# Fifteen early score operands in the weight slots, and layer 2's preparation in its written order

## Chip, core and metric

The kernel runs on one core of a Trainium2 chip. The metric is the device time of one execution in microseconds (us); a matrix engine (TensorE, PE in the rows), a vector engine (VectorE, DVE), a scalar engine (ScalarE, ACT) and the DMA queue of SyncE (SP) do the work.

## What is computed

Windowed attention with 32 global tokens, then two feed-forward layers on the 2304 resulting tokens of width 512:

```
s_l  = scale * q_l @ k_l.T masked to |i - j| <= 32, and scale * q_l @ k_g.T beside it
a_l  = softmax(s_l);  out_l = a_l @ [v_g, v_l];  out_g the same over all keys
x    = [out_g, out_l], heads side by side                        # 2304 x 512
h    = x @ w_in                                                  # 512 x 2048
g    = h where h >= 1, 0 where h <= -1, (h + 1)^2 / 4 between
x1   = g @ w_out                                                 # 2048 x 512
out  = ((x1 @ w_a) * (x1 @ w_b)) @ w_out2                        # 512 x 1536, 1536 x 512
```

The weights arrive as 64-bit numbers. Every factor of the two layers is split into a high and a low part, so that each product takes three matmuls (high by high, low by high, high by low).

## The kernel before

**Attention.** The tokens are cut into 18 blocks of 128, and the work on them into items (one block, one pair of heads); three items make a group (`Local`). For an item a transfer brings `qk` (176 KB; L176) and one brings `v` (256 KB; L183). A group goes through scores on TensorE (`s_pe`, L203), minimum on VectorE (L218), exponential on ScalarE (L223), sum and reciprocal (`recip`, L230, L231), scaling (`scale`: one half on ScalarE, L239, one on VectorE, L240), transposition (`t_pe`, L246, copied at L248) and the product with `v` (`v_pe`, L257).

**Layer 1.** Three blocks make a tile, so there are six. A unit (t, f) of tile t and one of 16 strips of the hidden width has an `h_unit` (matmuls `hp`, L587 to L589; ScalarE L915; VectorE L916, L917; the split of the gate at L920, L921) and an `x_unit` (matmuls into four `acc` banks on the same lines). A raw weight strip (`wraw`, 512 KB, loaded at L101) is turned into fp32 at L109 (ScalarE), L110 and L111 (VectorE), and split at L118 (high part, ScalarE) and L119 (low part, VectorE; L117 to L119 are the general `split`). Strips are named i0, i1, ... for `w_in` and o0, o1, ... for `w_out`, used in the order i0, i1, o0, i2, o1, ...

**The start.** `begin` asks for the first transfers in the order of a string, `EARLY`: k is the next item's `qk`, v its `v`, w the next raw weight strip. All of them go to SP's queue, but for two `qk`. The pool of 32 slots called "w" holds split weights; at the start they are empty, and raw weights as well as the first twelve `qk` and `v` live in them (`EARLY_ITEMS`). Later items use pools of their own, so that item 12's `qk` and those behind it need a buffer of `qk`, and item 17's needs one that group 4's scores give back. Then `begin` runs groups 0 to 3 (tile 0), and the scores of group 4. The first six units of layer 1 on tile 0 (`FA`) run while tile 1's groups, 4 and on, go through attention between them.

**Layer 2.** Three stages s of 12 units; unit u = 12 s + f. Units 0 to 23 are `ab_unit`s: seven products k = 0 to 6 of three-matmul sums each (`prod`, L777 to L780), of which 0, 2, 4 and 5 go into bank `pb` and 1, 3 and 6 into bank `px`. VectorE and ScalarE take them out: L806 reads product 1, L816 and L817 products 4 and 3, L821 the last of `pb`, L825 product 6, L826 ends the second half. Product 0 of the next unit can't begin before L821 is done, product 3 not before L806, product 6 not before L817. Between products come fills: matmuls of the output layer for the unit before (`y_block`, bank `py`).

`side(u)` is called behind each product and prepares what comes: the loads `x1_load` for the next stage (at f = 1), `x_pre` (L646, L647; at f = 10, k = 6), `x_op` with its splits (at f = 11, one per k, L658 and L661 within), the sums of weights `ab_sum` (L686 to L689) and their splits `ab_split` for the next unit, the load `ab_load` for the one after, `y_prep` (a conversion and a split, in stage 0), and in stage 1 `yw_load`, `yw_sum` (L758 to L761, tile `yq`) and `yw_split` (tile `yo`). A scheduler places the instructions on each engine; it takes what it thinks ready first, and may so lift a step ahead of work that was written before it. `tc.issue_after(i)` keeps everything inside it behind instruction i.

Of the kernel before, what the change touches and what calls it, by code (L numbers as in the profile page):

```python
# [46 lines left out]

WARM = 6
START_GROUPS = 4
EARLY_ITEMS = 12  # L50
EARLY = "kkkkkkkkkvvvkkkwvvvwvvvwkkkvvvwkkvvvwwvvww"
FA = 6
LEAD1 = 2

# [8 lines left out]
QKBUFS = 5  # L63
# [5 lines left out]
def body(tc, qk, vw, kg, vg, vt, w1i, w1o, w2a, w2b, w2o, mask, eye, out):  # L69
    nc = tc.nc  # L70
# [24 lines left out]
    def w_load(key, src):  # L95
        if len(wraws) < EARLY.count("w"):
            raw = wp.tile([P, 512, 2], I32, name="wraw0", tag="w", bufs=32)
        else:
            raw = sp["p"].tile([P, 512, 2], I32, name="wraw", bufs=sp["raw"])
        wraws.append(key)  # L100
        nc.sync.dma_start(raw, src.bitcast(I32).rearrange("p (f two) -> p f two", two=2))  # L101
        wq.append((key, raw))
# [60 lines left out]
    class Item:  # L163
# [4 lines left out]
        def load(self):  # L168
            n = nat["n"]
            nat["n"] += 1  # L170
            if n < EARLY_ITEMS:
                self.qk = wp.tile([P, QK], F32, name="qk0", tag="w", bufs=32)
            else:
                self.qk = gp["k"].tile([P, QK], F32, name="qk", tag="qk", bufs=QKBUFS)
            queue = nc.scalar if n in (1, 3) else nc.sync
            queue.dma_start(self.qk, qk[self.blk, self.p])  # L176

        def load_v(self):
            if ld["v"] < EARLY_ITEMS:
                self.v = wp.tile([P, NQ, P], F32, name="v0", tag="w", bufs=32)  # L180
            else:
                self.v = ap.tile([P, NQ, P], F32, name="v", tag="v", bufs=VBUFS)
            nc.sync.dma_start(self.v, vw[self.blk, self.p])  # L183
# [187 lines left out]
    for t, blks in enumerate(TILES):  # L371
        loc = [(j, blk) for j, blk in enumerate(blks) if blk != GLOB]
        its = [Item(j, blk, p) for p in range(NPAIR) for j, blk in loc]
        n = len(loc) if len(loc) > 1 else 2
# [4 lines left out]
    ld = {"k": 0, "v": 0, "s_done": 0, "v_done": 0, "vb": 0, "g": 0}  # L379
    flat_items = [(g, it) for g in groups for it in g.items]  # L380
    first_glob = next(n for n, (g, it) in enumerate(flat_items) if isinstance(g, Glob))
# [12 lines left out]
    def load_v():  # L394
        g, it = flat_items[ld["v"]]
        it.load_v()
        ld["v"] += 1
        ld["vb"] += (ld["v"] > EARLY_ITEMS) + isinstance(g, Glob)

    def may_k():  # L400
        n = ld["k"]
        if n >= len(flat_items):
            return False
        if n >= first_glob:
            return "p" in gp and ld["s_done"] >= n
        return n < max(EARLY_ITEMS, ld["s_done"]) + QKBUFS

    def may_v():
        n = ld["v"]
        if n >= len(flat_items):  # L410
            return False
        need = (n >= EARLY_ITEMS) + (n >= first_glob)
        return (n < first_glob or "p" in gp) and ld["vb"] + need <= VBUFS

    def loads():
# [77 lines left out]
    def begin():  # L493
        for kind in EARLY:
            {"k": load_k, "v": load_v, "w": lambda: W1.load_to(W1.li + 1)}[kind]()
        n = START_GROUPS
        g = groups
        s_part(g[0])
        g[0].s_post()
        s_part(g[1])  # L500
        fill(WARM)
        low = []
        for k in range(n + 1):
            if k:
                for i in range(3):
                    g[k - 1].t_pe(i)
            if k + 1 < n:
                g[k + 1].s_post()
            if k + 2 < n:
                s_part(g[k + 2])  # L510
            if pend:
                low.pop()()
                w_end()
            if k < n:
                g[k].recip()
                g[k].scale()
            if k:
                v_part(g[k - 1])
                if k < n:
                    fill(WARM)  # L520
                else:
                    s_part(g[n])
                g[k - 1].v_post()
            if low:
                low.pop()()
            if k:
                low.append(x_chunk(0, k - 1, widths(0)))
            if k == n - 1:
                w_begin()
        low.pop()()  # L530
        w_begin()
        g[n].s_post()
        w_end()
# [4 lines left out]
    for g, grp in enumerate(groups):  # L538
        if g < START_GROUPS:
            continue  # L540
        n = grp.nt if isinstance(grp, Local) else 1
# [80 lines left out]
    def x1_load(s):  # L622
        n = half_cols(s)
        t0, t1 = PAIRS[s]
        w0 = widths(t0)
        for h in range(2):
            for c in range(NC):
                r = mp.tile([P, 384], F32, name=f"x1r{h}{c}", tag=f"xh{c}" if h else f"xraw{c}", bufs=1)
                lo, hi = h * n, (h + 1) * n
                if lo < w0:  # L630
                    e = min(hi, w0)
                    nc.sync.dma_start(r[:, :e - lo], x1d[t0][c, :, lo:e])
                if hi > w0:
                    b0 = max(lo, w0)
                    nc.sync.dma_start(r[:, b0 - lo:n], x1d[t1][c, :, b0 - w0:hi - w0])
                if s == 0 and h == 0:
                    q = t_tile("part", c % 2, c // 2)
                    nc.sync.dma_start(q, part[c])
                    nc.vector.tensor_tensor(r, r, q, ALU.add)
                xr[(h, c)] = r  # L640

    def x_pre(s):
        n = half_cols(s)
        for c in range(2):
            t1, t2 = t_tile("t1", c, 0), t_tile("t2", c, 1)
            nc.vector.tensor_tensor(t1[:, :n], xr[(1, c)][:, :n], xr[(0, c)][:, :n], ALU.subtract)  # L646
            nc.vector.tensor_tensor(t2[:, :n], xr[(1, 2 + c)][:, :n], t1[:, :n], ALU.subtract)  # L647
            tt[(1, c)], tt[(2, c)] = t1, t2

    def x_op(s, k):  # L650
        n = half_cols(s)
        if len(xo) <= k:
            xo.append((slot(), slot()))
        hi, lo = xo[k]
        for c in range(2):
            if k == 4:
                t3 = t_tile("t3", c, 0)
                nc.vector.tensor_tensor(t3[:, :n], xr[(1, 2 + c)][:, :n], xr[(1, c)][:, :n], ALU.subtract)  # L658
                tt[(3, c)] = t3
            if k == 5:  # L660
                nc.vector.tensor_tensor(tt[(2, c)][:, :n], xr[(0, 2 + c)][:, :n], tt[(2, c)][:, :n], ALU.subtract)  # L661
            src = [xr.get((0, c)), xr.get((0, 2 + c)), tt.get((2, c)), tt.get((1, c)), tt.get((3, c)),
                   tt.get((2, c)), xr.get((1, 2 + c))][k]
            split(hi[:, c, :n], lo[:, c, :n], src[:, :n])
# [15 lines left out]
    def ab_sum(u):  # L680
        if (u, 2) in wt:
            return
        a, b = wt[(u, 0)], wt[(u, 1)]
        q = sp["p"].tile([P, 4, 256], F32, name="wsum", bufs=1)
        h0, h1 = slice(0, 256), slice(256, 512)
        nc.vector.tensor_tensor(q[:, 1], b[:, h0], b[:, h1], ALU.add)  # L686
        nc.vector.tensor_tensor(q[:, 0], q[:, 1], a[:, h0], ALU.subtract)
        nc.vector.tensor_tensor(q[:, 2], a[:, h0], b[:, h0], ALU.subtract)
        nc.vector.tensor_tensor(q[:, 3], a[:, h1], q[:, 0], ALU.subtract)  # L689
        wt[(u, 2)] = q  # L690
        if u < U1:
            nc.sync.dma_start(wqd[u], q.rearrange("p a b -> p (a b)"))
# [43 lines left out]
    def y_prep(f):  # L736
        key, t = w2_conv()
        assert key == ("y", f)
        nc.sync.dma_start(yd[f // 2][:, f % 2], t)
        w = slot()  # L740
        split(w[:, 0], w[:, 1], t)
        wslots[key] = w
# [220 lines left out]
    for u in range(len(units)):  # L963
        for kind in (0, 1):
            if kind == 0:
# [17 lines left out]
                if u in conv_at:  # L983
                    i = conv_at.index(u)
# [58 lines left out]
    def side(u):  # L1043
        s, f = divmod(u, NF2)

        def run(k):
            if f == 1 and k == 0:
                x1_load(s + 1)
            if f == NF2 - 2 and k == 6:
                x_pre(s + 1)  # L1050
            if f == NF2 - 1:
                x_op(s + 1, k)
            if u > 0:
                if k == 1:
                    ab_sum(u + 1)
                elif 2 <= k < 6:
                    ab_split(u + 1, k - 2)
            if k == 6 and u + 2 not in (U1 + 1, U2 + 1):
                ab_load(u + 2)
            if k == 4 and s == 0:  # L1060
                y_prep(f)
            if s == 1:
                c = f // 2
                if f % 2 == 0:
                    if k == 0 and f == 0:
                        yw_load(0)
                    elif k == 6:
                        yw_sum(c)
                        if c < 5:
                            yw_load(c + 1)  # L1070
                elif k in (2, 5):
                    yw_split(c, k // 3)
        return run
# [19 lines left out]
    n = half_cols(2)  # L1093
# [235 lines left out]
```

## Time and profile before

| | us |
|---|---|
| three runs | 895.35, 899.59, 900.65 (median 899.59) |
| the profiled run | 902.1 |
| its span, first to last instruction | 900.3 |
| TensorE busy | 879.7 (98%) |
| VectorE busy | 633.8 (70%) |
| ScalarE busy | 488.9 (54%) |

The mean granted clock of TensorE is 0.991 of full speed. Busy times are of the profiled run; they overlap between engines, so the time is read from the engine that is waited for, and from what it waits for.

### The profile page before, as it was taken

How to read it: one execution, taken by the hardware profiler on the slowest of the kernel's cores; microseconds unless marked ns; L12 is line 12 of the kernel's file. 1: busy time of each engine (PE TensorE's matmuls, PEld its weight loads, DVE VectorE, ACT ScalarE, POOL GpSimd, SP SyncE). 2: the span in 40 equal slices, each digit the busy share in tenths (PEclk: the TensorE clock that was granted, in tenths of full speed). 3: DMA queues.
4: the chain of work that ended last, by engine and by line, in shares of the span. 5: the costliest groups of instructions: out<-in, count | busy, mean ns of one | idle time of the engine just before them, and what ended most of it. 6: DMA issues, size and time to landing. Idle time of an engine off the chain costs nothing.

```text
span 900.3 us, 19284 instructions
## 1 busy us (share of the span) xinstructions
PE 879.7 (98%) x7322; PEld 831.9 (92%) x7322; DVE 633.8 (70%) x1590; ACT 488.9 (54%) x1195; POOL 0.3 (0%) x5
## 2 busy tenths in 40 slices
PE   8699999999999999999999999999999999999998
PEld 6589999999999999988999999999989899999998
DVE  6599897666556655555488687776978668676683
ACT  6588676545445444443455555555745446555442
POOL 0000000000000000000000000000000000000000
PEclk9789999999999999999999999999999999999999
DMA  9948667855444532344282564533598521644531
GB/s 316 362 139 269 185 212 243 263 179 188 159 141 129 177 111 88 121 137 146 88 282 80 161 190 155 163 118 110 171 325 273 197 82 36 205 137 130 182 120 54
DMA packets 77612, 153.59 MB, mean 171 GB/s; under 512 B 9296, under 2 KB 35792, under 8 KB 77520
## 3 DMA queue, kind: packets, MB, share of 16 engines
q1 hardware_dynamic: 76944, 151.85, 51.8%
q8 instruction: 57, 0.93, 0.4%
q10 hardware_dynamic: 576, 0.52, 0.2%
q14 instruction: 35, 0.29, 0.1%
HBM read 119.05 MB, written 33.29 MB: 169 GB/s over the span
## 4 chain that ended last, share of the span: by engine, by line
PE 83%; DMA 8%; ACT 4%; DVE 3%; issue 1%; SPq 1%; ACTq 0%; DVEq 0%
PE hp L587 6%; PE acc L587 6%; PE acc L588 6%; PE acc L589 6%; PE hp L588 6%; PE hp L589 6%; PE pb L777 4%; PE pb L779 4%; PE pb L780 4%; PE py L844 3%; PE py L845 3%; PE px L777 3%; PE py L843 3%; PE px L779 3%; PE px L780 3%; DMA wraw<-in_w1i_dram 3%
## 5 line engine op out<-in xcount | busy, mean ns | idle before, releaser
L587 PE MATMUL hp<-xh,w 128*128 128x384 f32 (+1 forms) x384 | 131.9, 344 | 0.5 <-DVE m L916 0.4
L587 PE MATMUL acc<-g,w 128*128 128x384 f32 (+1 forms) x384 | 127.4, 335 | 1.7 <-ACT g L920 1.1
L588 PE MATMUL hp<-xh,w 128*128 128x384 f32 (+1 forms) x384 | 126.8, 330 | 1.0 <-DVE w L119 1.0
L589 PE MATMUL hp<-xl,w 128*128 128x384 f32 (+1 forms) x384 | 126.6, 330 | 0.0
L588 PE MATMUL acc<-g,w 128*128 128x384 f32 (+1 forms) x384 | 126.3, 329 | 0.0
L589 PE MATMUL acc<-g,w 128*128 128x384 f32 (+1 forms) x384 | 126.3, 329 | 0.0
L916 DVE SCALAR_TENSOR_TENSOR m<-hp,r 128x384 f32<-128x384 f32 (+1 forms) x96 | 51.1, 532 | 82.4 <-ACT r L915 82.3
L915 ACT ACTIVATE r<-hp,half 128x384 f32<-128x384 f32 (+1 forms) x96 | 53.8, 560 | 85.8 <-PE hp L589 82.6
L118 ACT ACTIVATE w<-wt 128x512 fp32r<-128x512 f32 (+1 forms) x94 | 53.5, 572 | 51.4 <-PE pb L780 31.0
L777 PE MATMUL pb<-w 128*128 128x384 f32 (+1 forms) x240 | 78.0, 325 | 3.3 <-DVE m L821 3.0
L920 ACT ACTIVATE g<-m 128x384 fp32r<-128x384 f32 (+1 forms) x96 | 48.4, 504 | 57.2 <-DVE m L917 57.1
L779 PE MATMUL pb<-w 128*128 128x384 f32 (+1 forms) x240 | 78.2, 326 | 0.0
L780 PE MATMUL pb<-w 128*128 128x384 f32 (+1 forms) x240 | 78.0, 325 | 0.0
L587 PEld LDWEIGHTS acc<-g,w 128*128 128x128 f32 x384 | 72.6, 190 | 3.5 <-ACT g L920 1.4
L587 PEld LDWEIGHTS hp<-xh,w 128*128 128x128 f32 x384 | 73.0, 190 | 2.8 <-DMA xh<-x0d 0.7
L588 PEld LDWEIGHTS hp<-xh,w 128*128 128x128 f32 x384 | 73.0, 190 | 1.8 <-DVE w L119 1.4
L589 PEld LDWEIGHTS hp<-xl,w 128*128 128x128 f32 x384 | 72.9, 190 | 0.8 <-DMA xl<-x0d 0.8
L589 PEld LDWEIGHTS acc<-g,w 128*128 128x128 f32 x384 | 72.9, 190 | 0.2
L588 PEld LDWEIGHTS acc<-g,w 128*128 128x128 f32 x384 | 73.0, 190 | 0.0
L921 DVE TENSOR_TENSOR g<-m,g 128x384 fp32r<-128x384 f32 (+1 forms) x96 | 51.1, 532 | 23.8 <-ACT g L920 23.4
L119 DVE TENSOR_TENSOR w<-wt,w 128x512 fp32r<-128x512 f32 (+1 forms) x94 | 57.6, 616 | 4.9 <-ACT w L118 3.9
L223 ACT ACTIVATE e<-e,mn 128x128 f32<-128x128 f32 x128 | 47.9, 390 | 14.6 <-DVE mn L218 14.4
(168 smaller groups left out, 2040.2 us busy)
## 6 DMA issues: line engine op xcount, KB each, us to landing
v<-in_vw_dram SPq DMA_DIRECT2D x64, 256.0 KB, 5.1
wt<-wd SPq DMA_DIRECT2D x50, 256.0 KB, 2.9
qk<-in_qk_dram SPq DMA_DIRECT2D x62, 176.0 KB, 4.1
wraw<-in_w1i_dram SPq DMA_DIRECT2D x16, 512.0 KB, 4.7
wraw<-in_w1o_dram SPq DMA_DIRECT2D x16, 512.0 KB, 4.0
wraw<-in_w2a_dram SPq DMA_DIRECT2D x12, 512.0 KB, 4.1
wraw<-in_w2b_dram SPq DMA_DIRECT2D x12, 512.0 KB, 4.0
wd<-wt SPq DMA_DIRECT2D x24, 256.0 KB, 2.2
```

Of the source, the lines that this page charges most:

```text
L118: nc.scalar.activation(hi, src, AF.Copy)
L119: nc.vector.tensor_tensor(lo, src, f32(hi), ALU.subtract)
L587: nc.tensor.matmul(acc, whi, xhi, start=first, stop=False)
L588: nc.tensor.matmul(acc, wlo, xhi, start=False, stop=False)
L589: nc.tensor.matmul(acc, whi, xlo, start=False, stop=last)
L777: nc.tensor.matmul(out[:, :n], w[:, 0, r], hi[:, c, :n], start=start and c == 0, stop=False, skip_group_check=True)
L779: nc.tensor.matmul(out[:, :n], w[:, 1, r], hi[:, c, :n], start=False, stop=False, skip_group_check=True)
L780: nc.tensor.matmul(out[:, :n], w[:, 0, r], lo[:, c, :n], start=False, stop=k in (1, 5, 6) and c == 1, skip_group_check=True)
L915: at["act"] = nc.scalar.activation(r[:, :W], hp[:, :W], AF.Relu, bias=half, scale=0.5 / W_UP).ins
L916: nc.vector.scalar_tensor_tensor(m[:, :W], hp[:, :W], 1.0 / W_UP, r[:, :W], ALU.mult, ALU.max)
L920: nc.scalar.activation(gh[:, :W], m[:, :W], AF.Copy)
L921: nc.vector.tensor_tensor(gl[:, :W], m[:, :W], f32(gh[:, :W]), ALU.subtract)
```

## The change

The count of items whose `qk` lives in weight slots goes from 12 to 15, that of `v` stays 12. The string gets three more k and another order: the first six items of tile 1 are asked for ahead of most raw weights. In `side(u)`, each call puts its steps behind the last VectorE and the last ScalarE instruction that stand at that point.

```diff
-EARLY_ITEMS = 12
-EARLY = "kkkkkkkkkvvvkkkwvvvwvvvwkkkvvvwkkvvvwwvvww"
+EARLY_K, EARLY_V = 15, 12
+EARLY = "kkkkkkkkkvvvkkkwvvvwvvvkkkvvvwkkkwwvvvwkkwvvw"
...
-            if n < EARLY_ITEMS:
+            if n < EARLY_K:
                 self.qk = wp.tile([P, QK], F32, name="qk0", tag="w", bufs=32)
...
-            if ld["v"] < EARLY_ITEMS:
+            if ld["v"] < EARLY_V:
                 self.v = wp.tile([P, NQ, P], F32, name="v0", tag="w", bufs=32)
...
-        ld["vb"] += (ld["v"] > EARLY_ITEMS) + isinstance(g, Glob)
+        ld["vb"] += (ld["v"] > EARLY_V) + isinstance(g, Glob)
...
-        return n < max(EARLY_ITEMS, ld["s_done"]) + QKBUFS
+        return n < max(EARLY_K, ld["s_done"]) + QKBUFS
...
-        need = (n >= EARLY_ITEMS) + (n >= first_glob)
+        need = (n >= EARLY_V) + (n >= first_glob)
...
         def run(k):
+            last = {i.engine: i for i in nc.cur_bb.bb.instructions}
+            with tc.issue_after(last[mybir.EngineType.DVE]), tc.issue_after(last[mybir.EngineType.Activation]):
+                beside(k)
+
+        def beside(k):
             if f == 1 and k == 0:
                 x1_load(s + 1)
```

Line numbers of layer 2's last stage grow by five. The first place is SP's queue in the start, from strip i2's load (before) and strip o0's (after) on. In the kernel before, the three `qk` of row 35 are those of items 17, 18 and 19:

```order
27 L101 DMA wraw_225<-in_w1i_dram 128x1024
28 L176 DMA qk<-in_qk_dram 128x352 x2
29 L183 DMA v<-in_vw_dram 128x512 x3
30 L101 DMA wraw_237<-in_w1o_dram 128x1024
31 L101 DMA wraw_239<-in_w1i_dram 128x1024
32 L183 DMA v<-in_vw_dram 128x512 x2
33 L101 DMA wraw_245<-in_w1o_dram 128x1024
34 L101 DMA wraw_247<-in_w1i_dram 128x1024
35 L176 DMA qk<-in_qk_dram 128x352 x3
```

In the changed kernel row 29 holds items 15, 16 and 17:

```order
28 L101 DMA wraw_223<-in_w1o_dram 128x1024
29 L176 DMA qk<-in_qk_dram 128x352 x3
30 L101 DMA wraw_231<-in_w1i_dram 128x1024
31 L101 DMA wraw_233<-in_w1o_dram 128x1024
32 L183 DMA v<-in_vw_dram 128x512 x3
33 L101 DMA wraw_241<-in_w1i_dram 128x1024
34 L176 DMA qk<-in_qk_dram 128x352 x2
35 L101 DMA wraw_247<-in_w1o_dram 128x1024
```

Item 17's `qk` moved ahead of i2, o1, i3, o2 and i4 and of five `v`.

The second place is VectorE in layer 2, unit 13 of the kernel before, where `x_pre(2)`'s two L646 stand between L817 and L821 of the unit:

```order
1225 L817 TENSOR_TENSOR m<-px,r 128x320
1226 L119 TENSOR_TENSOR w<-wsum,w 128x256
1227 L646 TENSOR_TENSOR t_9482<-x1r_8509,x1r_8501 128x384
1228 L646 TENSOR_TENSOR t_9486<-x1r_8511,x1r_8503 128x384
1229 L821 SCALAR_TENSOR_TENSOR m<-m,pb 128x320
```

In the changed kernel they stand in unit 22, ahead of unit 23's L806, together with both L647 and the sums of `yq`:

```order
1356 L119 TENSOR_TENSOR g<-m,g 128x320
1357 L646 TENSOR_TENSOR t_9482<-x1r_8509,x1r_8501 128x384
1358 L646 TENSOR_TENSOR t_9486<-x1r_8511,x1r_8503 128x384
1359 L647 TENSOR_TENSOR t_9483<-x1r_8513,t_9482 128x384
1360 L647 TENSOR_TENSOR t_9487<-x1r_8515,t_9486 128x384
1361 L758 TENSOR_TENSOR yq<-yin 128x256
1362 L760 TENSOR_TENSOR yq<-yin 128x256
1363 L759 TENSOR_TENSOR yq<-yq,yin 128x256
1364 L806 TENSOR_TENSOR m<-px,r 128x320
```

Behind them come unit 23's steps, whose end differs as well; before, from L817 to L821:

```order
1379 L817 TENSOR_TENSOR m<-px,r 128x320
1380 L119 TENSOR_TENSOR w<-t_9576,w 128x384
1381 L119 TENSOR_TENSOR w<-t_9580,w 128x384
1382 L661 TENSOR_TENSOR t_9483<-x1r_8505,t_9483 128x384
1383 L821 SCALAR_TENSOR_TENSOR m<-m,pb 128x320
```

and after:

```order
1377 L817 TENSOR_TENSOR m<-px,r 128x320
1378 L658 TENSOR_TENSOR t_9576<-x1r_8513,x1r_8509 128x384
1379 L658 TENSOR_TENSOR t_9580<-x1r_8515,x1r_8511 128x384
1380 L119 TENSOR_TENSOR w<-wsum,w 128x256
1381 L119 TENSOR_TENSOR w<-t_9576,w 128x384
1382 L119 TENSOR_TENSOR w<-t_9580,w 128x384
1383 L119 TENSOR_TENSOR w<-wt,w 128x256
1384 L821 SCALAR_TENSOR_TENSOR m<-m,pb 128x320
```

Two subtractions of `x_op` and two splits of the next unit's weights moved in between.

The third place is VectorE in unit 11, the end of stage 0. Before, behind product 1's L806:

```order
1166 L806 TENSOR_TENSOR m<-px,r 128x384
1167 L119 TENSOR_TENSOR w<-x1r_7100,w 128x320
1168 L119 TENSOR_TENSOR w<-wt,w 128x512
1169 L119 TENSOR_TENSOR w<-t_8183,w 128x320
```

In the changed kernel:

```order
1154 L806 TENSOR_TENSOR m<-px,r 128x384
1155 L119 TENSOR_TENSOR w<-x1r_7098,w 128x320
1156 L119 TENSOR_TENSOR w<-x1r_7100,w 128x320
1157 L686 TENSOR_TENSOR wsum<-wt 128x256
1158 L688 TENSOR_TENSOR wsum<-wt 128x256
1159 L687 TENSOR_TENSOR wsum<-wsum,wt 128x256
1160 L817 TENSOR_TENSOR m<-px,r 128x384
1161 L689 TENSOR_TENSOR wsum<-wt,wsum 128x256
1162 L119 TENSOR_TENSOR w<-t_8183,w 128x320
```

`ab_sum` for unit 12, which stood in the unit before, moved into unit 11, and L817 ahead of most of `x_op`.

## Rows read from the trace of the kernel before

**Rows 1.** Page's busy line; windows: length, busy per engine, clock, DMA share, GB/s.
```profile
PE 879.7 (98%) x7322; PEld 831.9 (92%) x7322; DVE 633.8 (70%) x1590; ACT 488.9 (54%) x1195; POOL 0.3 (0%) x5
...
25.00:31.00 6.00, 5.90 (x132) 5.17 (x130) 4.69 (x11) 3.06 (x8) 0.00 (x0) 1.00 0.96 307
...
33.00:34.00 1.00, 0.00 (x0) 0.00 (x0) 0.00 (x0) 1.00 (x5) 0.00 (x0) 0.69 1.05 410
34.00:50.00 16.00, 10.35 (x58) 9.07 (x59) 9.57 (x36) 9.43 (x29) 0.00 (x0) 0.50 0.78 290
...
95.00:600.00 505.00, 504.45 (x4357) 479.86 (x4357) 346.44 (x897) 267.35 (x669) 0.00 (x0) 1.00 0.51 162
```

**Rows 2.** TensorE's waits over the span: us in total, times, longest.
```profile
PE s L203 <- DMA qk<-in_qk_dram: 7.9, 4, 6.8
PE pb L777 <- DVE m L821: 3.0, 2, 1.5
...
PE pb L777 <- ACT r L816: 0.3, 1, 0.3
```

**Rows 3.** Timeline of TensorE, 30 to 51 us: start, us, instruction, idle before.
```profile
30.62 0.64 PE L203 MATMUL s<-qk 64*32 64x128 f32 x16
38.06 1.63 PE L203 MATMUL s<-qk 64*32 64x128 f32 x32 [6.80 <-DMA qk<-in_qk_dram]
...
41.27 0.69 PE L588 MATMUL hp<-xh,w 128*128 128x384 f32 x1 [0.96 <-DVE w L119]
...
46.65 1.65 PE L587 MATMUL acc<-g,w 128*128 128x384 f32 x4 [0.64 <-ACT w L118]
```

**Rows 4.** The chain of waits that ended last, around 30 us: start, us, what.
```profile
30.08 7.94 DMA qk<-in_qk_dram
```

**Rows 5.** Timeline of ScalarE, 33 to 54 us.
```profile
33.30 0.61 ACT L118 ACTIVATE w<-wt 128x512 fp32r<-128x512 f32 x1
...
40.74 0.99 ACT L239 ACTIVATE e<-e,sm 128x128 f32<-128x128 f32 x3 [6.37 <-DVE sm L231]
...
43.94 1.22 ACT L109 ACTIVATE wt<-wraw 128x512 f32<-128x512 f32 x2
...
51.16 0.38 ACT L248 ACTIVATE pt<-tp 128x256 f32<-128x256 f32 x1 [1.36 <-PE tp L246]
...
53.65 0.58 ACT L915 ACTIVATE r<-hp,half 128x384 f32<-128x384 f32 x1 [0.78 <-PE hp L589]
```

**Rows 6.** Timelines of VectorE and TensorE, 659 to 703 us.
```profile
659.97 1.03 DVE L646 TENSOR_TENSOR t<-x1r,x1r 128x384 f32<-128x384 f32 x2 [2.43 <-DMA x1r<-x1d]
...
661.45 0.41 PE L777 MATMUL pb<-w 128*128 128x320 f32 x1 [1.48 <-DVE m L821]
...
700.70 0.42 DVE L758 TENSOR_TENSOR yq<-yin 128x256 f32<-128x256 f32 x1 [2.49 <-DMA yin<-yd]
...
702.25 0.41 PE L777 MATMUL pb<-w 128*128 128x320 f32 x1 [1.53 <-DVE m L821]
```

**Rows 7.** Timelines of TensorE and VectorE in unit 12.
```profile
639.90 0.31 PE L777 MATMUL pb<-w 128*128 128x320 f32 x1
...
643.82 0.42 DVE L758 TENSOR_TENSOR yq<-yin 128x256 f32<-128x256 f32 x1
644.16 0.41 DVE L760 TENSOR_TENSOR yq<-yin 128x256 f32<-128x256 f32 x1
...
647.61 0.68 DVE L119 TENSOR_TENSOR yo<-yq,yo 128x512 fp32r<-128x512 f32 x1
648.20 0.48 DVE L821 SCALAR_TENSOR_TENSOR m<-m,pb 128x320 f32<-128x320 f32 x1
```

**Rows 8.** Timelines of VectorE and TensorE, units 22 to 24.
```profile
750.24 0.49 DVE L825 TENSOR_TENSOR r<-px,r 128x320 f32<-128x320 f32 x1
...
764.36 0.55 DVE L1138 TENSOR_TENSOR m<-px,r 128x384 f32<-128x384 f32 x1
...
754.07 0.31 PE L777 MATMUL px<-w 128*128 128x320 f32 x1
```

## The prediction

> **What bounds the kernel now.** I read the page's busy line first: TensorE is busy 879.7 of 900.3 us [rows 1]. The windows say where the rest is: 505 us in the middle lose half a microsecond, so only the ends of the kernel can give anything back [rows 1]. The list of waits names what is left: 6.8 us in one piece for a `qk` transfer, 3.0 us in two pieces on VectorE's L821 [rows 2]; the others are about 1 us or less each. The same windows show a second cost of the first piece: the granted clock is 1.00 until 33 us and 0.50 from 34 to 50 us, so matmuls there run at half speed [rows 1].
>
> The first piece: group 5's scores begin at 30.62, run 16 records (items 15 and 16, first half) and stop until 38.06 [rows 3]. The chain of waits goes through the `qk` transfer issued at 30.08 that took 7.94 us [rows 4]: item 17's, which stands in SP's queue behind all of the early raw weights and values. Behind it VectorE and ScalarE wait in their own order: ScalarE's scaling of group 4 comes at 40.74, 6.37 us late, behind VectorE's reciprocal L231, which stands behind group 5's reductions [rows 5]. So a late transfer for group 5 holds group 4 and the weights too.
>
> The other two pieces: VectorE sits 2.43 us at 659.97 on a `x1r` load for `x_pre(2)`, and 2.49 us at 700.70 on a `yin` load [rows 6]. Both instructions were lifted ahead of L821, and TensorE waits for L821 to free bank `pb`, 1.48 and 1.53 us [rows 6].
>
> **Part 1, the transfer.** Ahead of item 17's `qk` in the new string are 17 `k`, 12 `v` and 3 `w`, against 17, 17 and 8 before: 5 values of 0.262 MB and 5 raw weights of 0.524 MB fewer, 3.9 MB. At 307 to 410 GB/s, the rates of 25 to 34 us [rows 1], that is 9.6 to 12.8 us: it lands at 25 to 28.5 instead of 38.02, and is needed at 31.0 after the first 16 records. I take it as in time. Items 12 to 14 now use weight slots, so item 17 no longer waits for group 4's scores either. What becomes later are raw weights: o0 to i4 stand behind three `k` more each. ScalarE's next reader of one after the scores is L109 at 43.94 [rows 5], some 6 us earlier in the new kernel, at about 37.5; with the same rates the first of them lands by about 30, the last at about 39, one per two microseconds, as they are read. I price that at nothing, and at up to 5 us as a rival.
>
> What then is late next: TensorE goes through group 5's scores without a break, to about 31.9 instead of 39.6. VectorE finishes group 4's six reductions at about 32 anyway and does group 5's in the next 1.3 us; then w(i1)'s low part needs the high part from ScalarE, which ends at 33.91 [rows 5] and is not moved. So L119 ends at 34.5, where it ended at 41.2, and the second unit's matmuls (41.27 with their wait) go 6.7 us earlier. ScalarE has the longer way: L915 follows and ends at 34.4, then three scalings (0.99) and six exponentials, which ended 3.2 us after the scaling's 40.74 and now end at 37.5 [rows 5]. From there to the first `acc` matmul is ScalarE's and VectorE's work, unchanged 2.6 us: 40.1 instead of 46.65 [rows 3]. The shift is **6.5 us**. It grows if the clock stays at 1.00: ScalarE's two later waits for TensorE, 1.36 and 0.78 us [rows 5], are waits for matmuls at half speed, and go; the end is 8.5. It shrinks if the clock falls: TensorE still stands some 3 us twice (31.9 to 34.5 with one matmul in it, and about 37 to 40), and in the kernel before the fall came 2 us after it stopped at 31.26 [rows 1, 3]. Then the `acc` matmuls take as long as before (1.65 us for four [rows 3]), and where the second unit and the first `acc` wait for splits once more, as at 41.27 and 46.65 (0.96 and 0.64 [rows 3]), 1.6 of the 6.5 are lost: 4.9, and 4.8 is my low end. I take 6.7, a little over the plain shift: one of the two gaps has a matmul in it, and each is half as long as the wait that stood before the fall.
>
> The Trainium skill, "TensorE: Matmul & The Clock Gate", section "HAM oscillation — how this bites in real kernels", describes bursts of matmuls whose waits for DMA send the engine back to the low clock each time. By that the shorter gaps here would be paid as well, and the sum would take the low end.
>
> **Part 2, the order beside layer 2.** `issue_after` pins each step behind the last VectorE and ScalarE instruction written so far. No instruction is added; TensorE's order is the same up to about 630 us. What it removes: `x_pre(2)` goes from unit 13 to unit 22, where its loads have long landed; the `yq` sums of L758 go behind the arithmetic of their unit. The waits for L821 (1.48 + 1.53) and 0.3 more for L816 go [rows 2, 6]: **3.3 us** gained; the least is 2.8, if L816's stays.
>
> What it adds: work that VectorE did early, in idle time, now falls at the ends of stages 0 and 1, where `x_op` alone nearly fills it. The price of an instruction is its distance to the next one: 0.335 for 128x256 (643.82 to 644.16), 0.60 for 128x512 (647.61 to 648.20) [rows 7], and in proportion 0.40 and 0.47 for 320 and 384 columns.
>
> Units 22 and 23: before, VectorE runs from L825 at 750.24 to L1138 at 764.36 without a break, 14.1 us, and TensorE is just not held up [rows 8]. The new order puts into the same stretch L646 and L647 twice each (1.9), four `yq` sums (1.3), two `yo` (1.2), and two 512 and three 256 weight splits (2.2): 6.6 more, 20.7 in all. Walking it: `x_pre` and three sums push L806 to 755.6, while TensorE would begin product 3, which overwrites the bank that L806 reads, at 754.07: 1.5 late. L817 ends at 761.9 and holds product 6 for 1.5 more, L821 ends at 764.9, where unit 24 could have begun at 760.45; L1138 comes at 770.8. TensorE loses **4.6 us** (3 to 5.5: the two products' waits and the bank's overlap in part, and ScalarE's splits may come later than I walk them).
>
> Units 11 and 12: VectorE is full there already with `x_op`. The new order adds `ab_sum` (1.3), one weight conversion (0.94) and a 512 split of `y_prep` (0.6) to the unit, and puts L817 behind only 2.3 us of them, so that VectorE waits there for product 4, about 1.7 us. L821 then ends at 642.6, where TensorE wants `pb` at 639.90 [rows 7]: 2.7 lost, and up to 1.5 at product 3 of the next unit. I take **3.5** (1.5 to 4.5), since one of the two is partly the other's.
>
> Unit 15: its weight splits now stand behind unit 14's arithmetic, and their loads in SP's queue behind `x1_load(2)`. Before, TensorE lost 0.3 there, behind L816 [rows 2]. I take 0.5 (0 to 1.5).
>
> **The sum.** 902.1 (the profiled run; its span is 900.3) − 6.7 − 3.3 + 4.6 + 3.5 + 0.5 = 900.7. The profiled run is 2.5 over the median of 899.6, so **898 us**. Ends: gain 8.5 + 3.3 against 3 + 1.5 + 0 is 7.3 faster, 892; gain 4.8 + 2.8 against 5.5 + 4.5 + 1.5 is 3.9 slower, 903.5.
>
> **Rivals.** (A) *The queues hide the written order.* TensorE has fills between products, and VectorE is done early in most units, so that the lumps at the stage ends cost nothing. For it: VectorE is busy 70% over the kernel [rows 1]. Against: the 14.1 us of work without a break at 750. Then 6.7 + 3.3 = 10 are gained: 889.5. (B), slower: *the raw weights become the late transfer.* SP's transfers of 512 KB asked for at 26 to 30 us now stand behind three more `k`, and the last three wait for slots that TensorE's early matmuls release. If each is read 1 us or more before it lands, ScalarE's L109 waits in its place for what L203 waited for. For it: the DMA share is 0.96 to 1.05 from 25 to 34 us [rows 1], so what one transfer gains others lose. From 5 us lateness it gives back all but 1.7 of the 6.7, and with layer 2's +5.3 the time is 899.6 + 3.6 = 903. (C) *It doesn't do what it says:* item 17's `qk` is still issued late, because SP's queue waits for earlier transfers to complete before it issues. Startup 0, layer 2 +5.3: 905.
>
> **Numbers.** Forecast 0.60 (892 to 903), A 0.16, B 0.17, C 0.07. About 1% is what a measurement of this kernel can tell from no change: 890.6 and 908.6. Faster: most of A and little of the forecast, 0.13; slower: parts of B and C, 0.03; within 0.84. The range takes in the forecast's and B and reaches to A's edge: 889 to 904.
>
> **What would show it.** Right: no wait of TensorE for `qk` over 1 us after 30, `acc` begins at about 40, the low clock lasts under 8 us; no wait for `x1r` or `yin` on VectorE; new waits of TensorE for L821, L817 or L806 around units 11 to 12 and 23 to 24, together 6 to 10 us. Wrong: stage ends without such waits (A), or ScalarE's L109 waiting for `wraw` at 35 to 45 (B).

## The result, and the profile after

The changed kernel takes 905.42 us (median of nine runs, 902.67 to 907.40), the kernel before 899.59 in as many (895.35 to 901.59): a ratio of 1.0066, interval 1.0046 to 1.0086. The change loses some 6 us where a gain of 1.6 was forecast, and ends 1.4 us above the range. The profiled run took 906.77, with a span of 905.0 (4.7 more than before).

Both kernels issue the same work on TensorE, 7322 matmuls, so the same matmul can be looked up in both traces. The difference of its start, after minus before:

| place | us | what lies between |
|---|---|---|
| 58 us | −6.4 | the start, 6.4 gained |
| 135 us | −6.0 | layer 1, 0.5 given back |
| 160 us to unit 11 | −3.9 | layer 1, 2.1 more given back |
| unit 13 | −0.7 | units 11 and 12, 3.2 lost |
| unit 14 | −2.3 | a wait that is gone, 1.6 |
| unit 18 | −3.8 | the second such wait, 1.5 |
| unit 23 | −3.7 | nothing |
| unit 24 | +1.7 | unit 23, 5.4 lost |
| end | +4.7 | unit 24 and behind, 3.0 lost |

**The start.** TensorE's timeline of the changed kernel answers to [rows 3], and the windows to [rows 1]:

```profile
30.77 0.86 PE L203 MATMUL s<-qk 64*32 64x128 f32 x24
32.09 0.86 PE L203 MATMUL s<-qk 64*32 64x128 f32 x24 [0.46 <-DVE mn L218]
34.12 0.69 PE L587 MATMUL hp<-xh,w 128*128 128x384 f32 x1 [1.17 <-ACT w L118]
...
40.32 1.65 PE L587 MATMUL acc<-g,w 128*128 128x384 f32 x4 [0.73 <-ACT w L118]
```

```profile
34.00:50.00 16.00, 15.10 (x143) 13.32 (x144) 13.31 (x34) 13.58 (x41) 0.00 (x0) 0.69 0.74 270
95.00:600.00 505.00, 502.69 (x4341) 477.25 (x4340) 335.59 (x871) 255.52 (x654) 0.00 (x0) 1.00 0.48 156
```

The 6.80 us in which TensorE waited for `qk` are gone, and `acc` begins at 40.32 instead of 46.65. Item 17's `qk` was issued at 21.01 and landed at 26.33. The clock still falls, but to a mean of 0.69 over these 16 us, not 0.50: it is 0.50 from 34 to 43 us and 1.00 from 44 on. The long middle, which had lost 0.55 us, now loses 2.31: 505 less the busy time.

**Layer 1.** The rows behind that, of ScalarE first and of TensorE then:

```profile
128.78 0.66 ACT L109 ACTIVATE wt<-wraw 128x512 f32<-128x512 f32 x1 [0.82 <-DMA wraw<-in_w1o_dram]
...
138.72 0.66 ACT L109 ACTIVATE wt<-wraw 128x512 f32<-128x512 f32 x1 [0.94 <-DMA wraw<-in_w1o_dram]
```

```profile
136.57 0.44 PE L587 MATMUL hp<-xh,w 128*128 128x384 f32 x1 [1.26 <-DVE m L916]
141.64 0.45 PE L587 MATMUL hp<-xh,w 128*128 128x384 f32 x1 [0.64 <-DVE xraw L270]
```

ScalarE waits for raw weights, and TensorE stands for 1.26 and 0.64 us behind VectorE in the same stretch. The wait at 138.72 is for the last raw strip of layer 1. The kernel before converts that strip at 142.90, and the row there shows no wait. Its transfer was issued at 134.28 and landed at 138.64, before at 139.25 and 142.82: it was asked for 5.0 us sooner and came 4.2 us sooner. So a TensorE that comes 6 us sooner gets ahead of transfers that didn't come 6 us sooner.

**Layer 2.** The list of TensorE's waits over the whole span, as [rows 2]:

```profile
PE pb L777 <- DVE m L821: 4.1, 2, 2.3
PE px L777 <- DVE m L817: 3.0, 1, 3.0
...
PE s L203 <- DMA qk<-in_qk_dram: 0.8, 3, 0.3
```

L821 still costs, but at other places: once in unit 11, once in unit 23. TensorE's timeline at both:

```profile
638.76 0.41 PE L777 MATMUL pb<-w 128*128 128x320 f32 x1 [2.32 <-DVE m L821]
...
759.11 0.41 PE L777 MATMUL px<-w,w 128*128 128x320 f32 x1 [3.01 <-DVE m L817]
...
762.05 0.69 PE L777 MATMUL pb<-w 128*128 128x384 f32 x1 [1.80 <-DVE m L821]
762.54 0.52 PE L779 MATMUL pb<-w 128*128 128x384 f32 x1
...
767.59 0.34 PE L777 MATMUL px<-w 128*128 128x384 f32 x1
```

And VectorE in the same place, where [rows 8] showed 14.1 us without a break:

```profile
749.40 1.02 DVE L646 TENSOR_TENSOR t<-x1r,x1r 128x384 f32<-128x384 f32 x2
...
752.28 0.48 DVE L806 TENSOR_TENSOR m<-px,r 128x320 f32<-128x320 f32 x1
...
753.02 1.96 DVE L119 TENSOR_TENSOR w<-x1r,w 128x384 fp32r<-128x384 f32 x4
...
758.57 0.49 DVE L817 TENSOR_TENSOR m<-px,r 128x320 f32<-128x320 f32 x1
758.97 1.02 DVE L658 TENSOR_TENSOR t<-x1r,x1r 128x384 f32<-128x384 f32 x2
...
761.51 0.49 DVE L821 SCALAR_TENSOR_TENSOR m<-m,pb 128x320 f32<-128x320 f32 x1
...
768.39 0.56 DVE L1143 TENSOR_TENSOR m<-px,r 128x384 f32<-128x384 f32 x1 [0.21 <-PE px L780]
```

From L646 on VectorE has hardly a gap until 768, and no row before L1143 waits for TensorE. Here TensorE waits, for 3.01 and 1.80 us. And there is a second price, in the windows:

```profile
755.00:760.00 5.00, 1.99 (x12) 1.50 (x10) 5.00 (x11) 0.69 (x2) 0.00 (x0) 1.00 0.26 105
760.00:765.00 5.00, 3.20 (x11) 2.75 (x10) 4.97 (x12) 3.52 (x10) 0.00 (x0) 0.56 0.36 108
765.00:770.00 5.00, 5.00 (x20) 4.26 (x19) 4.03 (x10) 2.20 (x7) 0.00 (x0) 0.75 0.34 131
```

The granted clock is 0.56 and 0.75 in unit 24, so a matmul of 384 columns takes 0.52 us at 762.54 and 0.34 at 767.59. Before, it was 1.00 throughout.

### The profile page after: what moved, and what is told of

Read it like the earlier page. It is cut to its first block, busy times and chain, and to the rows that moved or that the text cites. A ratio compares the mean times of both kernels' runs of the same rounds, so it can differ in the third digit from the quotient of the medians.

```text
span 905.0 us, 19186 instructions
## 1 busy us (share of the span) xinstructions
PE 885.5 (98%) x7322; PEld 834.4 (92%) x7322; DVE 635.5 (70%) x1590; ACT 480.6 (53%) x1195; POOL 0.3 (0%) x5
## 3 DMA queue, kind: packets, MB, share of 16 engines
HBM read 119.05 MB, written 33.29 MB: 168 GB/s over the span
## 4 chain that ended last, share of the span: by engine, by line
PE 82%; DMA 6%; DVE 5%; ACT 5%; issue 1%; SPq 0%; ACTq 0%; DVEq 0%
PE acc L587 6%; PE hp L587 6%; PE acc L588 6%; PE acc L589 6%; PE hp L589 6%; PE hp L588 6%; PE pb L777 4%; PE pb L779 4%; PE pb L780 4%; PE px L777 3%; PE py L844 3%; PE py L845 3%; PE py L843 3%; PE px L779 3%; PE px L780 3%; PE o L257 2%
## 5 line engine op out<-in xcount | busy, mean ns | idle before, releaser
L118 ACT ACTIVATE w<-wt 128x512 fp32r<-128x512 f32 (+1 forms) x94 | 53.1, 569 | 25.1 <-DVE wt L111 23.3
```

Source lines behind the costliest of these rows:

```text
L118: nc.scalar.activation(hi, src, AF.Copy)
```

## The experiments

The theory after the result, T: part 1 gains, part 2 loses more than that; it loses because VectorE's steps stand in a lump at the stage ends, where TensorE waits for L817 and L821 and then runs at the low clock. The rivals: the two parts hurt each other in layer 1 and in the DMA queues; or the splits on ScalarE, not VectorE, are what is held back. All kernels that contain part 1 have the same instructions up to layer 1's last tile, but for four matmuls of `mid_fill`. Each ratio is to runs of the kernel before from the same session, whose medians lie between 899.6 and 900.7. The column "layer 2" is the time from unit 0's first matmul to the end in the profiled run, against 397.1 us of the kernel before.

| kernel | median (runs) | ratio, interval | layer 2 |
|---|---|---|---|
| changed | 905.42 (9) | 1.0066, 1.0046 to 1.0086 | +8.6 |
| `start_only` | 898.05 (10) | 0.9965, 0.9947 to 0.9984 | −0.8 |
| `order_only` | 910.47 (4) | 1.0120, 1.0090 to 1.0150 | +10.7 |
| `xpre_early` | 902.26 (10) | 1.0016, 0.9996 to 1.0037 | +4.7 |
| `pin_two` | 899.52 (10) | 0.9990, 0.9971 to 1.0009 | +1.9 |
| `hold_clock` | 907.63 (4) | 1.0075, 1.0055 to 1.0096 | +7.7 |
| `pin_mid` | 894.24 (4) | 0.9933, 0.9910 to 0.9955 | −1.4 |
| `pin_act` | 898.31 (10) | 0.9980, 0.9963 to 0.9998 | +0.8 |
| `pin_dve` | 906.11 (4) | 1.0066, 1.0045 to 1.0087 | +9.7 |
| `slots_only` | 900.41 (10) | 1.0011, 0.9991 to 1.0031 | −1.8 |
| `mid_fill` | 895.93 (12) | 0.9961, 0.9939 to 0.9982 | −0.7 |

**Part 1 alone** (`start_only`: the changed kernel without the wrapper in `side`).

```diff
         def run(k):
-            last = {i.engine: i for i in nc.cur_bb.bb.instructions}
-            with tc.issue_after(last[mybir.EngineType.DVE]), tc.issue_after(last[mybir.EngineType.Activation]):
-                beside(k)
-
-        def beside(k):
```

> Part 1 alone (string and 15 weight slots), layer 2 as before. Theory T (the loss sits at the ends of layer 2's stages and is part 2's): the start gives 6.4 us, layer 1 gives back about 2.5 as in the changed kernel's trace, layer 2 as before: 3.9 faster than before, about 895.7 (ratio 0.9955). Rival R (starting early makes later transfers collide, part 2 is harmless): no gain, 899 to 905.

It is 0.35% faster. In its profiled run the shift against the kernel before stood at −6.5 at 58 us, and −3.3 at 160. The two waits for L821 are still there, with 1.50 and 1.10 us.

**Part 2 alone** (`order_only`: the kernel before with those lines).

> Part 2 alone, start as before. T: the two waits of 1.5 us for L821 go (3.3), the stage ends cost 3.2 and 8.4 as in the changed kernel's trace: 8.3 slower than before, about 908 (ratio 1.009), slower than the changed kernel. R: 3.3 faster, about 896.

It is 1.2% slower, without any edit of the start: the loss belongs to the written order. The waits are those of the changed kernel, this row first of them:

```profile
640.63 0.41 PE L777 MATMUL pb<-w 128*128 128x320 f32 x1 [2.33 <-DVE m L821]
```

**The place of `x_pre`** (`xpre_early`: the changed kernel with `x_pre` two units sooner, the rest pinned as it was).

```diff
-            if f == NF2 - 2 and k == 6:
+            if f == NF2 - 4 and k == 6:
```

> The changed kernel with x_pre two units earlier (unit 8 and 20 instead of 10 and 22), still in written order. T: the lump at each stage end is 1.6 and 1.9 us smaller, and TensorE loses at least that much less: 3.5 us faster than the changed kernel, about 902; more if TensorE's clock then holds at unit 24. Rival: the waits come from which step stands in front of which (ScalarE's and VectorE's waits for one another), not from the sum of work: no change, 905.

It takes 3.2 us less than the changed kernel by the medians, and the intervals lie apart. What moves is the load on VectorE, and the wait for L817 shrinks from 3.01 to 1.08, while L821's stays, as TensorE's timeline shows:

```profile
752.28 0.42 PE L777 MATMUL px<-w,w 128*128 128x320 f32 x1 [1.08 <-DVE m L817]
755.22 0.44 PE L777 MATMUL pb<-w 128*128 128x384 f32 x1 [1.80 <-DVE m L821]
```

**Which engine's order costs** (`pin_act` keeps the `issue_after` on ScalarE, `pin_dve` that on VectorE).

```diff
-            with tc.issue_after(last[mybir.EngineType.DVE]), tc.issue_after(last[mybir.EngineType.Activation]):
+            with tc.issue_after(last[mybir.EngineType.Activation]):
                 beside(k)
```

> The changed kernel with the steps held behind ScalarE's last instruction alone; VectorE's part may be lifted as before. T (VectorE's work at the stage ends): VectorE's order is nearly that of before, most of the 11.6 us go, about 897 to 900. Rival (ScalarE's order, as its wait of 4.3 us for L658 in unit 23 of the changed kernel could suggest): as the changed kernel, 905.

> The changed kernel with the steps held behind VectorE's last instruction alone; ScalarE's part may be lifted. T: the lumps are on VectorE as in the changed kernel, 904 to 906. Rival (ScalarE's order): about 897 to 900.

VectorE's order alone costs as much as both (+9.7 in layer 2 against +8.6). ScalarE's alone costs +0.8 in all: unit 23 is 2.2 us longer there than in the kernel before, and units 13 to 17 are 3.3 us shorter. The rows of `pin_dve` repeat those of the changed kernel:

```profile
637.38 0.42 PE L777 MATMUL pb<-w 128*128 128x320 f32 x1 [1.75 <-DVE m L821]
...
758.23 0.41 PE L777 MATMUL px<-w,w 128*128 128x320 f32 x1 [2.88 <-DVE m L817]
...
761.32 0.69 PE L777 MATMUL pb<-w 128*128 128x384 f32 x1 [1.42 <-DVE m L821]
```

**Only the steps that wait for loads** (`pin_two`: only `x_pre` and `yw_sum` are held behind what is written before them; the rest is placed by the scheduler).

```diff
...
             if f == NF2 - 2 and k == 6:
-                x_pre(s + 1)
+                after_last(x_pre, s + 1)
...
                     elif k == 6:
-                        yw_sum(c)
+                        after_last(yw_sum, c)
```

> Part 1, and of part 2 only x_pre and the sums of yq put behind what is written before them; ab_sum, the weight splits, y_prep and x_op may be lifted as before. T: the waits for loads go (3.3), of the stage-end lumps only x_pre (1.6 and 1.9) and one set of yq sums (1.3) are left, at a cost of 0 to 4: start 6.4 less 2.5, layer 2 between 3.3 faster and 1 slower: 892 to 897. R: as the changed kernel, 903 to 906.

A miss: no gain that can be measured against the kernel before, and 1.5 more than part 1 alone by the medians, with intervals that overlap. TensorE's waits are smaller but still there: 1.35 us for L816 at 666.01, 1.1 in three pieces at 751 to 758, and 0.91 at 789. The three pieces come where `x_pre`, held at the stage's end, still stands in front of `x_op`; what makes the other two is not shown.

**The same, with `x_pre` in mid-stage** (`pin_mid`: as `pin_two`, but `x_pre` at f = 6).

```diff
...
-            if f == NF2 - 2 and k == 6:
-                x_pre(s + 1)
+            if f == 6 and k == 6:
+                after_last(x_pre, s + 1)
```

> Part 1, and of part 2 only x_pre and the yq sums kept behind what is written before them, x_pre moved to the middle of a stage (unit 6 and 18), everything else free to be lifted. T (the lumps of VectorE's work at the stage ends are the cost): no wait of TensorE over 0.5 us in units 10 to 24, the three waits of before (3.3) gone, 3 faster than with part 1 alone, 894 to 896. Rival (the order as such costs, wherever it is held): as the version with only the two steps held, 899 to 900.

This is the fastest kernel: 0.67% under the kernel before, 1.2% under the changed one (894.24 against 905.42), and 0.32% under `start_only`, where the intervals overlap a little. `mid_fill` below, the same kernel with four small matmuls more, came to 0.39% under the kernel before in twelve runs, so a lead over `start_only` is not shown. In the list of its waits over layer 2 nothing is above 0.6 us, and in the windows around unit 23 TensorE is busy throughout at full clock:

```profile
PE pb L777 <- ACT r L816: 0.6, 1, 0.6
```

```profile
745.00:750.00 5.00, 5.00 (x31) 4.74 (x32) 5.00 (x12) 2.85 (x8) 0.00 (x0) 1.00 0.27 107
750.00:755.00 5.00, 5.00 (x28) 4.52 (x27) 4.87 (x11) 4.10 (x12) 0.00 (x0) 1.00 0.44 133
```

VectorE is as busy in these windows (5.00 and 4.87 of 5 us) as in the changed kernel, so its busy share doesn't tell the two apart. What does is the work in its queue ahead of L821: from unit 22's L825 to unit 23's L821, idle time left out, beside the time from unit 23's first matmul to unit 24's.

| kernel | VectorE's work, us | unit 23, us |
|---|---|---|
| before, `start_only`, `slots_only` | 8.9 | 9.62 |
| `pin_mid`, `mid_fill` | 9.5 | 9.88 |
| `pin_act` | 11.0 | 11.81 |
| `pin_two` | 11.3 | 11.43 |
| `xpre_early` | 12.4 | 13.15 |
| changed, `order_only` | 14.2 | 15.03, 15.02 |
| `pin_dve` | 14.3 | 15.05 |

The unit grows with the amount of work that stands there (but for one pair in the middle), whichever steps make it up: the order costs by what it puts into the lump. Of the 6.0 us that 0.67% are, layer 2 holds 1.4 in the profiled run; the larger part is the start, whose gain this execution kept through layer 1, as told below.

**The clock behind the waits** (`hold_clock`: the changed kernel with matmuls of a zero operand in the two waits of unit 23, which add zero to a bank and change no result).

```diff
+        hold(u, 12)
         prod(u, 6, px, False)
...
         side(6)
+        hold(u, 7)
...
+    def hold(u, n):
+        if u != U2 - 1:
+            return
+        pe = [i for i in nc.cur_bb.bb.instructions if i.engine == mybir.EngineType.PE][-1]
+        with tc.issue_after(pe):
+            for _ in range(n):
+                nc.tensor.matmul(bank[("y", 4)], z, wslots[("y", NF2 - 2)][:, 0], start=False, stop=False)
...
```

> The changed kernel with 12 matmuls by a zero operand (512 columns, added to an open bank, so they change no sum) ahead of unit 23's product 6 and 7 behind it, where TensorE waits for L817 and L821. If the low clock at the start of unit 24 comes from these waits and is a cost of its own: the granted clock stays at 1.00 from 755 to 770 us, the waits for VectorE are filled and not shortened, and the kernel gets about 2.5 faster than the changed one, 903. If the waits alone are the cost: no change, 905 to 906.

The windows of this kernel over unit 24, beside those of the changed one above:

```profile
760.00:765.00 5.00, 4.03 (x20) 3.16 (x20) 5.00 (x13) 0.99 (x2) 0.00 (x0) 1.00 0.29 113
765.00:770.00 5.00, 5.00 (x26) 4.45 (x25) 4.96 (x12) 5.00 (x13) 0.00 (x0) 1.00 0.39 110
```

The clock is 1.00 where it was 0.56 and 0.75, and the same 9.6 us of work, from unit 24's first matmul on, take 2.75 us less. That is the price of the fall. Later the kernel gives back 1.2 of it in a wait for ScalarE at 796.40, so layer 2 is 0.9 shorter. The total isn't: this kernel came to layer 2 at −1.1 instead of −3.9, with the same instructions until there. Its profiled execution was late already at layer 1's first matmul (33.29, in the changed kernel 28.49), behind a wait for `qk` of 2.06 us at 13.64 where the changed kernel has one of 0.29, and with a mean clock of 0.83 up to 31 us instead of 1.00. So the local price is shown, a gain of the whole kernel is not.

**The transfer: buffer or place in the queue** (`slots_only`: the kernel before with fifteen `qk` in weight slots, and the old string).

```diff
-EARLY_ITEMS = 12
+EARLY_K, EARLY_V = 15, 12
 EARLY = "kkkkkkkkkvvvkkkwvvvwvvvwkkkvvvwkkvvvwwvvww"
```

> The kernel before with 15 early qk in weight slots and the old string: item 17's qk no longer needs a buffer that group 4's scores free, but stands behind the same raw weights and values as before. T (the place in the queue makes it late): TensorE waits 5 to 7 us for it as before, 899 to 901. Rival (the slot made it late): the wait is under 1 us, 895 to 898.

No difference, and TensorE's wait stays:

```profile
37.21 1.63 PE L203 MATMUL s<-qk 64*32 64x128 f32 x32 [5.37 <-DMA qk<-in_qk_dram]
```

Item 17's `qk` was issued at 29.55 here, at 30.08 before and at 29.59 in `order_only`, which has neither the slots nor the new string. In the changed kernel it was 21.01. Of the two halves of part 1, the place in SP's queue is what moves the start; a free buffer alone does nothing.

**The low clock at the start** (`mid_fill`: `pin_mid` with four warm-up matmuls behind group 5's scores).

```diff
...
+    def first_piece():
+        piece(START_GROUPS + 1, None)()
+        pe = [i for i in nc.cur_bb.bb.instructions if i.engine == mybir.EngineType.PE][-1]
+        with tc.issue_after(pe):
+            fill(HOLD)
...
-    atoms = [piece(START_GROUPS + 1, None)]
+    atoms = [first_piece]
```

> The version with x_pre in mid-stage, and four 128x128 matmuls on the identity (about 1.1 us) behind group 5's scores, where TensorE waits 1.2 us for the split of strip i1. If that wait brings the clock down at 33 to 34 us and the low clock costs on the way: the granted clock stays at 1.00 over 33 to 50, ScalarE's later waits for TensorE (1.25 and 0.80) shrink, up to 2 faster than that version, 892 to 894. If ScalarE's chain sets the pace in any case: no change, 894 to 895.

The clock stays at 1.00 from 33 to 44 us, but `acc` isn't earlier for it: TensorE reaches it sooner and waits longer, and the clock falls then (0.72 over 44 to 50).

```profile
44.30 0.96 PE L594 MATMUL acc<-g,w 128*128 128x384 f32 x4 [2.86 <-ACT w L119]
```

That is L118 of the other kernels, ScalarE's high part of the split. From layer 1's first matmul to `acc` this execution takes 11.86 us, that of `pin_mid` 11.83, with a clock of 0.66 over 33 to 37: up to `acc` ScalarE's chain sets the pace, and the low clock hides in it. In `acc`'s own matmuls it doesn't. `pin_mid` runs them at 1.00:

```profile
40.42 0.96 PE L587 MATMUL acc<-g,w 128*128 128x384 f32 x4 [1.62 <-ACT w L118]
```

From this row to the next `hp` matmul it takes 2.25 us. The changed kernel, at low clock there, begins `acc` at the same time (40.32) and takes 3.80; `mid_fill`, whose clock falls halfway, takes 2.79. So the filled wait moved the low clock and didn't remove it, and the medians show no gain (895.93 against 894.24, intervals that overlap).

## Why the prediction was wrong

The terms, as they were written and as they came, profiled run against profiled run:

| term | predicted | measured |
|---|---|---|
| start | −6.7 | −6.4 |
| waits gone | −3.3 | −3.1 |
| units 11 and 12 | +3.5 | +3.2 |
| unit 15 | +0.5 | 0.0 (a wait of 0.2, made up in unit 16) |
| units 22 to 24 | +4.6 | +8.4 |
| layer 1 | 0 | +2.5 (between 58 and 160 us) |
| sum | −1.4 | +4.6, against a span that is 4.7 longer |

Each measured term is a difference of two shifts from the table at the head, so they add up to the end's shift but for what small pieces lie between.

**The start was right in its mechanism; its size is less sure.** Item 17's `qk` landed at 26.33, where 25 to 28.5 was worked out. No `qk` wait over 0.3 us is left, and `acc` begins at 40.32, where 40.1 was worked out. But the 6.4 is the difference to one execution of the kernel before. `order_only` and `slots_only`, which ask for item 17 as late as it does, stood at −2.6 and −2.5 at 58 us, 1.6 of it because their clock was 1.00 in `acc`. Against these two the new string gains about 3.9. The forecast then took 2.5 off, since the profiled run lay so far over its median; as far as these two executions tell, that 2.5 lay in the start, and the start's term had removed it already. The changed kernel's profiled run lies 1.35 over its own median. So that step makes some 1.2 of the 7.4 us between the 898 forecast and 905.42, and the terms make the rest.

The clock fell, as the low end had it, and for about 10 us, where under 8 was named as a sign. Up to `acc` that cost nothing, since ScalarE's splits, scalings and exponentials are the longer way; in `acc` itself it cost 1.55 us, 3.80 against the 2.25 of `pin_mid`. The kernel before paid the same there (1.65 us for its first four), so the difference of the two doesn't show it. The Trainium skill, "TensorE: Matmul & The Clock Gate", section "HAM oscillation — how this bites in real kernels", describes bursts of matmuls whose waits for DMA send the engine back to the low clock. The trace shows the same fall at the start (a mean of 0.69) and at unit 24 (0.56), here behind waits for VectorE and ScalarE; it is paid for where TensorE itself is the bound, in `acc` and at unit 24.

**The step that failed** is the one that says of units 22 and 23 "TensorE loses 4.6 us (3 to 5.5...)". The mechanism was there: VectorE's lump holds up TensorE. The walk of its queue put unit 24's start 4.5 us late, and it came 5.4 late, 4.8 of it in two waits. In the parts the walk was off: of its three waits of some 1.5 the first, product 3's behind L806, did not come, since TensorE's new order has product 4 and four fill matmuls ahead of product 3 (L806 at 752.28, product 3 at 753.03); L817's wait was 3.01 instead. What the walk left out is what TensorE does after such waits. It came back at half clock, and lost another 3.0 behind unit 24's start, of which `hold_clock` gives 2.75 to the clock. The start's term had the clock in it; this one hadn't.

**A term put at nothing** is layer 1's. The prediction priced the later raw weights at nothing, and its reason reached only to the first strips, which land by 39 us. So it took a shift at 58 us to be a shift at 160. Nothing in the kernel before spoke of a loss there, where the middle lost half a microsecond [rows 1]. How much comes back differs from one execution to the next of the same instructions: at 160 us the profiled runs stand at −1.0 (`hold_clock`), −2.6 (`pin_two`), −2.9 (`mid_fill`), −3.3 (`start_only`), −3.9 (changed), −5.8 (`pin_dve`), −6.5 (`pin_act`), −7.3 (`xpre_early`) and −7.6 (`pin_mid`). In `hold_clock`, `mid_fill` and `pin_two` a part of it is missing at 58 us already (−3.1, −2.5 and −5.6). A spread of 6.5 us is more than any term of layer 2 but one, and a profile of one execution can't price it.

**The rivals.** A, that the queues hide the written order, is out: TensorE waited for L821 and L817 at the stage ends, and `pin_dve` against `pin_act` shows that VectorE's order is what does it. B, the raw weights as the late transfer, came in another place: no L109 waits for `wraw` at 33 to 48 us. At 138 one does, and 2.5 us came back between 58 and 160: if that wait is the cause, it is B's mechanism with half its price and 100 us later. C is out: item 17's `qk` was issued 9 us sooner, and the wait for it is gone.

The two waits for loads were worth less than the 3.3 of their term. In `pin_mid` both are gone, and units 13 and 17 are 1.6 and 1.5 us shorter than in the kernel before, but 1.8 are lost elsewhere, so that its layer 2 is 1.4 shorter. `slots_only` and `start_only`, which keep the free order, have −1.8 and −0.8 with such waits still in them, one of 1.1 us and two of 1.5 and 1.1. So the two waits of 1.5 were partly one execution's luck, and no run here shows that holding those steps in mid-stage makes layer 2 shorter than the free order does.

**What stays open.** What layer 1 gives back, from 58 to 160 us, goes roughly with ScalarE's wait for the last raw strip:

| kernel | given back | that wait | its transfer, issue to landing |
|---|---|---|---|
| `start_only` | 3.2 | 2.48 | 5.93 |
| `pin_two` | 3.1 | 1.19 | 4.70 |
| changed | 2.5 | 0.94 | 4.36 |
| `hold_clock` | 2.1 | 1.24 | 4.81 |
| `pin_dve` | 2.0 | none | 3.61 |
| `pin_act` | 0.5 | none | 3.56 |
| `xpre_early` | 0.3 | none | 3.59 |
| `pin_mid` | 0.3 | 0.18 | 3.63 |
| `mid_fill` | −0.3 | none | 3.62 |

In the kernel before the transfer took 3.57. Where ScalarE waits long, it isn't asked for late; it takes longer. `pin_dve` doesn't fit, and an earlier wait of 1.44 at 107.48 in `pin_mid` cost it nothing. So the cause is argued, not shown, and why the transfer takes longer in some executions is open. A third buffer for raw weights would tell; it wasn't tried. Nor is it settled why `hold_clock`'s runs are no faster than the changed kernel's.

## What to carry to other kernels

Written order isn't better or worse than a scheduler's; what matters is how much work stands ahead of the instruction that frees a buffer. A step that waits for a load is better held back to the middle of a stage, where the engine has room, than to the stage's end, where it joins the lump. That this beats the scheduler's own order is not shown here. Price a wait of TensorE with the clock that follows it where TensorE is the bound, and price a gain ahead of a stretch that transfers feed as not yet safe until that stretch is through.

## What the runs showed of the hardware

A TensorE wait has a tail, but not always. After waits of 3.01 and 1.80 us the granted clock was 0.56 and 0.75 in two windows of 5 us. At the start of the changed kernel it fell behind waits of no more than 0.46 and 1.17 us (0.81 over 33 to 34, 0.50 over 34 to 43). After one wait of 2.32 us at 638.76 in the changed kernel it stayed 1.00; after one of 2.33 us at the same instruction in `order_only` it fell to 0.78 (640 to 643) and 0.65 (643 to 646), and unit 12 took 12.30 us instead of 10.78. The length of the wait alone doesn't say which.

One and the same sequence of instructions came out 6.5 us apart at 160 us, though the granted clock from 95 us on was 1.00 in all of these executions. In this kernel a difference under 1% needs many runs (with ten, the interval of `start_only` is 0.37% wide), and a profile of each kernel only says where its own execution spent the time.
